# Two weight conversions moved by one batch each, and vector work queued behind the softmax low part

## The chip, the cores and the metric

One NeuronCore of a Trainium2 chip runs the kernel. The metric is device time in microseconds (us); lower is better. The time of a kernel is the median of its runs.

## The reference

Four batches (B = 4) of 576 tokens go through an attention with 32 memory slots and then through two feed-forward networks, all in fp32.

```python
# attention, 8 heads of 64
a = softmax(phi)                       # over 32 memory slots
k_m, v_m = a^T k, a^T v                # 32 x 64 per head
attn = softmax(q k_m^T / 8)
x = (attn v_m) as (2304 tokens, 512)
# first network
h = max(x @ moe_w_in, 0);   x = (h * h) @ moe_w_out
# second network
h = x @ moe2_w_in
g = h * tanh(log1p(exp(min(h, 20))))   # for h > 20: h * tanh(h)
out = g @ moe2_w_out
```

Both `w_in` are 512 x 2048, both `w_out` 2048 x 512.

## The kernel before

**Numbers in two parts.** Every large matrix product is made as three products of parts: a high part (rounded to the type that TensorE multiplies fast) and a low part (what the rounding left). high x high, high x low and low x high add up in PSUM; so each product shows three lines of matmuls (L471 to L473 for the first layer of network one, L433 to L435 for its second layer, L780 to L782 and L755 to L757 for network two).

**Weights have to be converted.** The four weight matrices arrive as 64-bit words. The class `Conv` turns them, in units of 128 x 512 values, into fp32 (and into high and low part). Network one's are called i1 and o1, network two's i2 and o2, 16 units each. A unit takes three ticks. In the first, ScalarE scales the high word in place (L192, the Prelu). In the second, VectorE joins the words (L214, L221, into `ct`), the raw buffer comes free and the next raw load is issued (L167). In the third, ScalarE rounds (L187) and VectorE makes the low part (L229). i2 and o2 are then stored to DRAM scratch from a staging tile (L231) and loaded again later (L713, `load_w2`), since SBUF has no room for them yet. The staging tiles have the tag `i1` with 4 buffers, which is also the tag of the pages of w_in1 that are loaded again for later batches (L592, `win1r`).

**Stages.** Attention (`kv_unit`, `attn_unit`) makes, for each batch and half batch of 288 tokens, the softmax part `at` (VectorE transpose L368), its high part `ah` (ScalarE, L375) and its low part `al` (VectorE, L376). `w_part` multiplies v_m into w_in1 (L386) and splits the result (`wp`, L392 and L393), so that the first layer reads ah, al and wp directly. `a_tile` runs the first network: for each of up to 16 blocks of d_ff (a step) six matmuls to `h`, ScalarE Relu (L479) and Square (L480), high part `g` (L484, or on VectorE for batch 3, L486), low part (L487, VectorE), and 12 matmuls that add to four accumulators, three steps later (`LAG`). Batches 0 and 1 are taken together in groups of 4, 6 and 6 blocks, 12 calls of `a_tile` numbered i = 0 to 11; the batches numbered 2 and 3 (the third and the last) follow with 16 blocks for each half. The second network then takes all tokens in 5 tiles of 512 or 384.

**Order.** A planner orders the instructions of each engine beforehand, from the order in which the code names them and from its own estimates of when operands are ready; an instruction may be moved far ahead of its place in the code. An engine then executes strictly in that order. `tc.issue_after(x)`, here in `behind(marks, key)`, keeps the instructions of its block behind x on x's engine, and adds no wait for anything else. `marks[b, half]` is a VectorE instruction of the softmax of that half batch. `c1.after` names the mark behind which the joining work of `Conv.fields` stays, for i1 and o1: (0,0) up to i = 0, (0,1) at i = 1, (1,0) at i = 2, (1,1) at i = 3 and none after. `kv_soft` puts the batch 2 maximum (L260) behind (1,1). `paced` puts the Prelu behind the latest Relu named (`marks["step"]`). All DMAs are issued by SyncE's queue, SP, one after another.

`c2` is the converter of the second network's weights: i2 and then o2, one unit started in two of three ticks, from the third group of batches 0 and 1 (once c1 is done) to the end of batch 2. While batch 3 runs, the 16 units of i2 and then those of o2 are loaded into their final places.

Of the kernel before, what the change touches and what calls it, by code (L numbers as in the profile page):

```python
# [8 lines left out]
F32 = mybir.dt.float32  # L9
F32R = mybir.dt.float32r  # L10
# [7 lines left out]
B, H, S, D, M = 4, 8, 576, 64, 32  # L18
DM, FF = 512, 2048
P = 128  # L20
# [4 lines left out]
NF = FF // P  # L25
# [4 lines left out]
LAG = 3  # L30
# [5 lines left out]
def body(tc, q, kvm, kvt, phi, w_in1, w_out1, w_in2, w_out2, out):  # L36
    nc = tc.nc
# [13 lines left out]
    dram = cm_dram.__enter__()  # L51
    cm_const, const = open_pool("const", "left")
    cm_wo, wo = open_pool("wo", "left")
    cm_pg, PG = open_pool("pg", "left")
    cm_x, X = open_pool("x", "left")
    cm_y, Y = open_pool("y", "right")
# [11 lines left out]
    for p in range(2):  # L68
        t = Y.tile([P, (NC + 1) * P], F32, name=f"phi{p}")
# [62 lines left out]
    wt = {}  # L132

    w1 = dram.tile([NPG, P, 4, 256], F32, name="w_i1")
    w2 = {key: dram.tile([NF, P, 2, 512], F32, name=f"w_{key}") for key in ("i2", "o2")}

    marks = {}
# [10 lines left out]
    class Conv:  # L150
# [20 lines left out]
        def tick(self, start=True, between=None):  # L171


            ends = [x for x in self.flight if x[2] == 2]
            bits = [x for x in self.flight if x[2] == 1]
            for x in ends:
                key, u = x[0], x[1]
                if key[1] == "2":
                    x[4] = Y.tile([P, 2, 512], F32R, tag="i1", name=f"st_{key}_{u}", bufs=4)
                    x[4] = [x[4][:, 0], x[4][:, 1], x[4]]  # L180
                else:
                    if (key, u // 2) not in wt:
                        wt[key, u // 2] = tuple(
                            wo.tile([P, 2, DM], F32R, tag=f"wo{part}{u // 2}", name=f"{key}{part}{u // 2}")
                            for part in "hl")
                    x[4] = [w[:, u % 2, :] for w in wt[key, u // 2]]
                nc.scalar.copy(x[4][0], x[3])  # L187
            if start and self.started < min(self.loaded, self.limit) and self.ready(*self.order[self.started]):
                key, u = self.order[self.started]
                high = self.raw[key, u][:, :, 1].bitcast(F32)  # L190
                with behind(marks, "step" if self.paced else None):
                    nc.scalar.activation(high, high, AF.Prelu, scale=2.0 ** -112, alpha=-2.0 ** 32)  # L192
                self.started += 1
                self.flight.append([key, u, 0, None, None])
            with behind(marks, self.after):
                self.fields(bits, ends, between)
            for x in self.flight:
                x[2] += 1
            for x in list(self.flight):
                if x[2] == 3 or (x[2] == 2 and x[0] == "i1"):  # L200
                    self.done.add((x[0], x[1]))
                    self.flight.remove(x)

        def fields(self, bits, ends, between):
            for x in bits:
                key, u, c = x[0], x[1], x[1] % 2
                if key == "i1":
                    if c == 0:
                        wt[key, u // 2] = Y.tile(
                            [P, 4, 256], F32, tag="i1", name=f"win1_{u // 2}", bufs=4)  # L210
                    x[3] = wt[key, u // 2][:, :, c * P:(c + 1) * P]
                else:
                    x[3] = X.tile([P, 512], F32, tag="ct", name=f"ct_{key}_{u}", bufs=2)
                nc.vector.tensor_scalar(  # L214
                    out=x[3].bitcast(I32), in0=self.word(x, 0), scalar1=29, scalar2=None,
                    op0=ALU.logical_shift_right)
            if between is not None:
                between()
            for x in bits:
                d = x[3].bitcast(I32)  # L220
                nc.vector.scalar_tensor_tensor(  # L221
                    out=d, in0=self.word(x, 1), scalar=3, in1=d,
                    op0=ALU.logical_shift_left, op1=ALU.bitwise_or)
                if x[0] == "i1" and x[1] % 2:
                    nc.sync.dma_start(w1[x[1] // 2], wt["i1", x[1] // 2])
                self.raw.pop((x[0], x[1]))
                self.load()
            for x in ends:
                nc.vector.tensor_sub(x[4][1], x[3], x[4][0].bitcast(F32))  # L229
                if x[0][1] == "2":  # L230
                    nc.sync.dma_start(w2[x[0]][x[1]], x[4][2].bitcast(F32))  # L231

        def word(self, x, i):
            t = self.raw[x[0], x[1]][:, :, i]
# [104 lines left out]
    def attn_unit(b, half, nxt=None):  # L339
        n = f"{b}{half}"  # L340
        qt = q_t.pop((b, half))
        ps = banks2(f"psc{n}")
        for g in range(4):
            for p in range(2):
                done_pe["psc", b, half] = nc.tensor.matmul(
                    ps[M * g:M * g + M, p, :T], kT[b][D * p:D * p + D, M * g:M * g + M],
                    qt[g // 2][D * p:D * p + D, g % 2, :], start=True, stop=True)
        if nxt is not None:
            nxt()

        x = Y.tile([P, 2, T], F32, tag="x", name=f"x{n}", bufs=1)
        xv = x.rearrange("p a (c m) -> p (a c) m", m=NB)
        for p in range(2):
            nc.vector.transpose(x[:, p], ps[:, p, :T])
        mx = Y.tile([P, 2 * TB], F32, tag="smx", name=f"smx{n}", bufs=1)
        marks[b, half] = nc.vector.tensor_reduce(out=mx, in_=xv, op=ALU.max, axis=AX.X)
        yield
        nc.vector.tensor_sub(xv, xv, mx.unsqueeze(2).to_broadcast([P, 2 * TB, NB]))
        nc.scalar.activation(x, x, AF.Exp)
        yield  # L360
        sm = Y.tile([P, 2 * TB], F32, tag="ssm", name=f"ssm{n}", bufs=1)
        nc.vector.tensor_reduce(out=sm, in_=xv, op=ALU.add, axis=AX.X)
        nc.vector.tensor_scalar_add(sm, sm, EPS)
        nc.vector.reciprocal(sm, sm)
        nc.vector.tensor_mul(xv, xv, sm.unsqueeze(2).to_broadcast([P, 2 * TB, NB]))
        yield
        a = Y.tile([P, 2, T], F32, tag="at", name=f"at{n}", bufs=1)
        marks[b, half] = nc.vector.transpose(  # L368
            a.rearrange("p a t -> p (a t)"), x.rearrange("p a t -> p (a t)"))
        pool = Y if b in (1, 2) else X  # L370
        a_t[b, half] = tuple(
            pool.tile([P, 2, T], F32R, tag=f"a{part}", name=f"a{part}{b}{half}", bufs=2)
            for part in "hl")
        hi, lo = a_t[b, half]
        nc.scalar.copy(hi, a)  # L375
        nc.vector.tensor_sub(lo, a, hi.bitcast(F32))  # L376
        yield

    wp = {}
# [116 lines left out]
    bounds = [sum(GROUPS[:i]) for i in range(len(GROUPS) + 1)]  # L496
# [73 lines left out]
    def attn_later(b, half):  # L570
        def nxt():
# [11 lines left out]

    subs = [(f0, f1, b, half) for f0, f1 in zip(bounds, bounds[1:])
            for b in range(2) for half in range(2)]
    c2 = Conv([("i2", u) for u in range(NF)] + [("o2", u) for u in range(NF)],
              lambda i: (Y, "raw", 3))

    def load_page(j):

# [4 lines left out]
    for i, (f0, f1, b, half) in enumerate(subs):  # L595
        final = i == len(subs) - 1
# [25 lines left out]
        def tick(fc):  # L622
            if len(c1.done) < 2 * NF:
                c1.tick()
            elif f0 == bounds[-2]:
                if not c2.loaded:
                    c2.load(3)
                c2.tick(start=fc % 3 != 2)

        def mid(fc):  # L630
            run_step(lanes, n_steps)
# [29 lines left out]


    def tick2(fc):
        c2.tick(start=fc % 3 != 2)

    b, nb = 2, 3
    lanes = [attn_later(b, 1), [[iter(range(2)), 2]] + kv_later(nb)]
# [25 lines left out]
    drain(*lanes)  # L693


    while len(c2.done) < 2 * NF:
        c2.tick()
    close(cm_psum2)
    cm_psum2 = tc.tile_pool(name="psum3", bufs=1, space=PSUM)
# [5 lines left out]
        tiles.append((c, n))  # L705
        c += n

    def load_w2(key, u):
        if key == "i2":
            t = Y2.tile([P, 2, 512], F32R, name=f"i2_{u}")  # L710
        else:
            t = wo.tile([P, 2, 512], F32R, tag=f"wo{'hl'[u % 2]}{u // 2}", name=f"o2_{u}")
        nc.sync.dma_start(t.bitcast(F32), w2[key][u])  # L713
        wt[key, u] = t

    y_raw, y_t = {}, {}

# [12 lines left out]
        nc.scalar.copy(hi, t)  # L730
        (nc.gpsimd if i else nc.vector).tensor_sub(lo, t, hi.bitcast(F32))  # L731

    def post0(fc):
        load_w2("i2", fc)

    def post1(fc):
        if fc >= 8 and fc % 2 == 0:
            load_y(0, fc // 2 - 4)
        elif fc >= 8:
            split_y(0, fc // 2 - 4)  # L740
        if fc >= LAG + 1 and fc % 2 == 0:
            load_w2("o2", fc - LAG - 1)
            load_w2("o2", fc - LAG)

    nothing = lambda fc: None
    acc_tags = ["mm", "b0", "bg1", "bg2"]
    a_tile(B - 1, 0, 0, NF, nothing, nothing, post0, acc_tags)
    a_tile(B - 1, 1, 0, NF, nothing, nothing, post1, acc_tags)


    def mm4_step(acc, fc, gh, gl, n, done):
# [18 lines left out]
    for i, (c0, n) in enumerate(tiles):  # L770
        acc = [psum.tile([P, 512], F32, tag=f"acc{d}", name=f"b{i}{d}") for d in range(n // P)]
        done = store_out(c0)
        for fc in range(NF):
# [9 lines left out]
            if step == 1:  # L783
                flush()
                run_pend(0)
                for c in range(NF):
                    if ("o2", c) not in wt:
                        load_w2("o2", c)
            u = X.tile([P, 512], F32, tag="ah", name=f"u{m}", bufs=2)[:, :n]
            nn = X.tile([P, 512], F32, tag="al", name=f"n{m}", bufs=2)[:, :n]  # L790
            nh = X.tile([P, 512], F32, tag="ys0", name=f"nh{m}", bufs=2)[:, :n]
# [80 lines left out]
```

## Time and profile before

| | |
|---|---|
| median of 3 runs | 811.53 us (810.93 to 815.98) |
| profiled execution | 809.73 us, its span 807.9 us |
| TensorE matmul (PE) busy | 776.5 us, 96% |
| VectorE (DVE) busy | 577.8 us, 72% |
| ScalarE (ACT) busy | 452.3 us, 56% |
| mean granted TensorE clock | 0.983 |
| DMA, mean | 138 GB/s over the span |

The profile is of one execution. The span runs from the first to the last instruction. PE, DVE, ACT and POOL are the busy rows of TensorE's matmuls, VectorE, ScalarE and GpSimd; PEclk is the granted TensorE clock, 1.00 being the upper of its two levels (2.4 GHz) and 0.50 the lower (1.2 GHz). A gap in front of an instruction is shown in brackets with what ended it.

### The profile page before, as it was taken

To read this page: it belongs to the slowest core of one execution; us is meant where nothing else is said; L and a number is where in the kernel's file an instruction comes from. 1 tells how busy PE (TensorE), PEld (TensorE's weight loads), DVE (VectorE), ACT (ScalarE), POOL (GpSimd) and SP (SyncE) were. 2 spreads that over 40 slices of the span, in tenths; PEclk is the share of its full clock that TensorE was granted. 3 is DMA by queue.
4 is the path that set the end of the run, shared out by engine and by line. 5 is a ranking of instruction groups with operands and counts; after the bars stand their busy time and mean duration, and the time that the engine had idled before them with its cause. 6 is when DMAs were issued, how large, how long until landed. Compare 5 with 4: busy or idle time off the path is not lost.

```text
span 807.9 us, 13777 instructions
## 1 busy us (share of the span) xinstructions
PE 776.5 (96%) x5288; PEld 676.5 (84%) x5288; DVE 577.8 (72%) x1022; ACT 452.3 (56%) x916; POOL 119.4 (15%) x104
## 2 busy tenths in 40 slices
PE   5797999999988999999999999999999999999997
PEld 4586898999777988999988888888888889999896
DVE  4988646785677883334588887888878887777774
ACT  3767766785657775334445445444564446555453
POOL 0000000000000000000223243222522242222222
PEclk7698999999999999999999999999999999999999
DMA  9991435699789977506630002000110001001001
GB/s 337 406 391 73 164 100 162 235 329 362 251 312 345 389 253 281 211 1 228 248 105 1 0 27 73 0 1 1 39 53 1 0 20 54 1 1 39 1 2 39
DMA packets 38705, 111.77 MB, mean 138 GB/s; under 512 B 3952, under 2 KB 10096, under 8 KB 38640
## 3 DMA queue, kind: packets, MB, share of 16 engines
q1 hardware_dynamic: 38640, 110.90, 37.8%
q8 instruction: 41, 0.67, 0.3%
q14 instruction: 24, 0.20, 0.1%
HBM read 80.48 MB, written 30.41 MB: 137 GB/s over the span
## 4 chain that ended last, share of the span: by engine, by line
PE 80%; DMA 8%; DVE 7%; ACT 3%; issue 1%; SPq 0%; ACTq 0%; DVEq 0%
PE hb L781 8%; PE hb L780 8%; PE hb L782 8%; PE b L756 8%; PE b L755 8%; PE b L757 8%; PE a L433 6%; PE a L435 6%; PE a L434 6%; DMA raw_i<-in_moe_w_in_dram 3%; PE h L471 3%; PE h L472 3%; PE h L473 3%; DMA w_i<-st_i 2%; PE pw L386 1%
## 5 line engine op out<-in xcount | busy, mean ns | idle before, releaser
L433 PE MATMUL a<-g,o1h 128*128 128x288 f32 x512 | 150.3, 301 | 3.0 <-ACT g L484 1.5
L434 PE MATMUL a<-g,o1l 128*128 128x288 f32 x512 | 149.2, 297 | 0.0
L808 POOL TENSOR_TENSOR gl<-nh,gh 128x512 fp32r<-128x512 f32 (+1 forms) x80 | 97.4, 1219 | 285.5 <-PE b L757 177.0
L435 PE MATMUL a<-g,o1h 128*128 128x288 f32 x512 | 134.8, 295 | 0.7 <-DVE g L487 0.7
L781 PE MATMUL hb<-yl,i 128*128 128x512 f32 (+1 forms) x320 | 118.9, 372 | 0.0
L780 PE MATMUL hb<-yh,i 128*128 128x512 f32 (+1 forms) x320 | 118.9, 372 | 0.0
L782 PE MATMUL hb<-yh,i 128*128 128x512 f32 (+1 forms) x320 | 118.8, 371 | 0.0
L804 DVE SCALAR_TENSOR_TENSOR n<-n,u 128x512 f32<-128x512 f32 (+1 forms) x80 | 79.5, 994 | 52.5 <-ACT u L800 52.5
L756 PE MATMUL b<-o,gh 128*128 128x512 f32 x288 | 113.6, 395 | 0.0
L755 PE MATMUL b<-o,gh 128*128 128x512 f32 x288 | 113.5, 394 | 0.0
L757 PE MATMUL b<-o,gl 128*128 128x512 f32 x288 | 112.4, 395 | 0.0
L433 PEld LDWEIGHTS a<-g,o1h 128*128 128x128 f32 x512 | 96.5, 189 | 11.1 <-ACT g L484 4.0
L794 ACT ACTIVATE u<-hb 128x512 f32<-128x512 f32 (+1 forms) x80 | 44.4, 555 | 107.5 <-PE hb L782 107.5
L434 PEld LDWEIGHTS a<-g,o1l 128*128 128x128 f32 x512 | 96.8, 189 | 1.3 <-issue 1.2
L479 ACT ACTIVATE s<-h 128x288 f32<-128x288 f32 x128 | 52.0, 410 | 79.9 <-PE h L473 78.4
L435 PEld LDWEIGHTS a<-g,o1h 128*128 128x128 f32 x512 | 90.7, 188 | 3.0 <-DVE g L487 1.6
L471 PE MATMUL h<-ah,wp 128*128 128x288 f32 x256 | 79.9, 313 | 5.3 <-ACT s L479 2.6
L472 PE MATMUL h<-al,wp 128*128 128x288 f32 x256 | 77.8, 304 | 5.3 <-DVE al L376 5.3
L487 DVE TENSOR_TENSOR g<-s,g 128x288 fp32r<-128x288 f32 x128 | 59.9, 469 | 32.2 <-ACT g L484 30.3
L731 POOL TENSOR_TENSOR yl<-yr,yh 128x512 fp32r<-128x512 f32 (+1 forms) x16 | 21.3, 1345 | 396.2 <-PE h L473 391.4
L807 ACT CAST gh<-nh 128x512 fp32r<-128x512 f32 (+1 forms) x80 | 46.3, 579 | 57.4 <-DVE nh L806 54.3
L473 PE MATMUL h<-ah,wp 128*128 128x288 f32 x256 | 77.1, 301 | 0.0
(98 smaller groups left out, 1393.4 us busy)
## 6 DMA issues: line engine op xcount, KB each, us to landing
raw_i<-in_moe_w_in_dram SPq DMA_DIRECT2D x32, 512.0 KB, 5.2
raw_o<-in_moe_w_out_dram SPq DMA_DIRECT2D x32, 512.0 KB, 7.7
win1r<-w_i SPq DMA_DIRECT2D x17, 512.0 KB, 5.8
w_i<-st_i SPq DMA_DIRECT2D x16, 512.0 KB, 4.5
w_o<-st_o SPq DMA_DIRECT2D x16, 512.0 KB, 6.8
i<-w_i SPq DMA_DIRECT2D x16, 512.0 KB, 7.7
o<-w_o SPq DMA_DIRECT2D x16, 512.0 KB, 4.1
kv<-in_kvm_dram SPq DMA_DIRECT2D x5, 1024.0 KB, 8.8
```

The costliest lines, as they stand in the source:

```text
L433: nc.tensor.matmul(o, wh[:, c, cs], sh, start=first, stop=False)
L434: nc.tensor.matmul(o, wl[:, c, cs], sh, start=False, stop=False)
L435: nc.tensor.matmul(o, wh[:, c, cs], sl, start=False, stop=last)
L471: nc.tensor.matmul(ph, w[:, 0, hg, fs], hi[:, hg], start=(hg == 0), stop=False)
L472: nc.tensor.matmul(ph, w[:, 0, hg, fs], lo[:, hg], start=False, stop=False)
L473: nc.tensor.matmul(ph, w[:, 1, hg, fs], hi[:, hg], start=False, stop=(hg == 1))
L755: nc.tensor.matmul(acc[t], gh[:, cs], wh, start=(fc == 0), stop=False)
L756: nc.tensor.matmul(acc[t], gh[:, cs], wl, start=False, stop=False)
L757: nc.tensor.matmul(acc[t], gl[:, cs], wh, start=False, stop=(fc == NF - 1))
L780: nc.tensor.matmul(h, wh[:, d * P:d * P + P], yh, start=(d == 0), stop=False)
L781: nc.tensor.matmul(h, wh[:, d * P:d * P + P], yl, start=False, stop=False)
L782: nc.tensor.matmul(h, wl[:, d * P:d * P + P], yh, start=False, stop=(d == 3))
```

## The change

- `c2` now holds o2 alone. Its first three raw loads are issued at the start of the last `a_tile` of batches 0 and 1 (i = 11); units start only in batch 2, one in every second step. Its staging is now two tiles of 128 x 512, high and low, with the tags `ys2` and `ys3` (2 buffers each; batches 0 and 1 used them for their sums), and each is stored by a DMA of its own (256 KB).
- A new converter `c3` holds i2. It runs during batch 3, one unit in every second step, with raw buffers in the pool `Y2`, and writes high and low part straight into the final tile. i2 is neither stored to scratch nor loaded from it.
- Both are `paced`.
- `marks[b, half]` is now the low part `al` (L376) and not the transpose (L368).

```diff
-    w2 = {key: dram.tile([NF, P, 2, 512], F32, name=f"w_{key}") for key in ("i2", "o2")}
+    w2 = dram.tile([NF, P, 2, 512], F32, name="w_o2")
...
-                if key[1] == "2":
-                    x[4] = Y.tile([P, 2, 512], F32R, tag="i1", name=f"st_{key}_{u}", bufs=4)
-                    x[4] = [x[4][:, 0], x[4][:, 1], x[4]]
+                if key == "i2":
+                    t = wt[key, u] = Y2.tile([P, 2, 512], F32R, name=f"i2_{u}")
+                    x[4] = [t[:, 0], t[:, 1]]
+                elif key == "o2":
+                    x[4] = [Y.tile([P, 512], F32R, tag=f"ys{i}", name=f"st{i}_{u}", bufs=2) for i in (2, 3)]
...
-                if x[0][1] == "2":
-                    nc.sync.dma_start(w2[x[0]][x[1]], x[4][2].bitcast(F32))
+                if x[0] == "o2":
+                    for i in range(2):
+                        nc.sync.dma_start(w2[x[1], :, i], x[4][i].bitcast(F32))
...
-        marks[b, half] = nc.vector.transpose(
-            a.rearrange("p a t -> p (a t)"), x.rearrange("p a t -> p (a t)"))
+        nc.vector.transpose(a.rearrange("p a t -> p (a t)"), x.rearrange("p a t -> p (a t)"))
...
-        nc.vector.tensor_sub(lo, a, hi.bitcast(F32))
+        marks[b, half] = nc.vector.tensor_sub(lo, a, hi.bitcast(F32))
...
-    c2 = Conv([("i2", u) for u in range(NF)] + [("o2", u) for u in range(NF)],
-              lambda i: (Y, "raw", 3))
+    c2 = Conv([("o2", u) for u in range(NF)], lambda i: (Y, "raw", 3))
+    c3 = Conv([("i2", u) for u in range(NF)], lambda i: (Y2, "raw", 3))
+    c2.paced = c3.paced = True
...
-            elif f0 == bounds[-2]:
-                if not c2.loaded:
-                    c2.load(3)
-                c2.tick(start=fc % 3 != 2)
+            elif final and not c2.loaded:
+                c2.load(3)
...
     def tick2(fc):
-        c2.tick(start=fc % 3 != 2)
+        c2.tick(start=fc % 2 == 0)
...
+    c3.load(3)
+
+    def tick3(fc):
+        c3.tick(start=fc % 2 == 0)
...
-    a_tile(B - 1, 0, 0, NF, nothing, nothing, post0, acc_tags)
-    a_tile(B - 1, 1, 0, NF, nothing, nothing, post1, acc_tags)
+    a_tile(B - 1, 0, 0, NF, tick3, nothing, nothing, acc_tags)
+    a_tile(B - 1, 1, 0, NF, tick3, nothing, post1, acc_tags)
+    while len(c3.done) < NF:
+        c3.tick()
```

## Rows read from the trace of the kernel before

**Rows 1.** The page, its first part: busy us of each engine.
```profile
PE 776.5 (96%) x5288; PEld 676.5 (84%) x5288; DVE 577.8 (72%) x1022; ACT 452.3 (56%) x916; POOL 119.4 (15%) x104
```

**Rows 2.** Busy time by stretch; after the engines PEclk, DMA share, GB/s.
```profile
70.00:80.00 10.00, 5.40 (x25) 4.93 (x24) 9.31 (x23) 6.19 (x15) 0.00 (x0) 0.67 0.02 8
170.00:262.00 92.00, 83.84 (x834) 74.15 (x833) 63.75 (x132) 60.36 (x137) 0.00 (x0) 1.00 0.90 324
221.50:320.00 98.50, 92.56 (x916) 82.22 (x917) 70.25 (x139) 68.10 (x154) 0.00 (x0) 1.00 0.86 318
320.00:400.00 80.00, 80.00 (x608) 79.15 (x593) 31.88 (x74) 33.42 (x78) 5.22 (x4) 1.00 0.48 172
```

**Rows 3.** Timeline of PE, 200 to 262 us: start, duration, gap and its releaser.
```profile
204.98 0.72 PE L345 MATMUL psc<-q,kT 64*32 64x288 f32 x16 [0.37 <-ACT kT L319]
...
221.53 0.40 PE L471 MATMUL h<-ah,wp 128*128 128x288 f32 x1 [1.09 <-ACT ah L375]
...
229.22 0.37 PE L433 MATMUL a<-g,o1h 128*128 128x288 f32 x1 [1.22 <-ACT st_i L187]
...
233.68 0.40 PE L433 MATMUL a<-g,o1h 128*128 128x288 f32 x1 [1.45 <-ACT g L484]
...
243.93 0.67 PE L386 MATMUL pw<-win1r,vT 64*32 64x256 f32 x16 [1.04 <-ACT et L282]
...
258.54 0.40 PE L471 MATMUL h<-ah,wp 128*128 128x288 f32 x1 [2.21 <-ACT s L479]
```

**Rows 4.** Timeline of ACT, the same stretch.
```profile
220.29 0.62 ACT L187 CAST st_i<-ct_i 128x512 fp32r<-128x512 f32 x1 [3.05 <-DMA win1r<-w_i]
...
240.38 0.68 ACT L192 ACTIVATE raw_o<-raw_o 128x512 f32<-128x512 f32 x1 [2.27 <-DMA raw_o<-in_moe_w_out_dram]
...
255.82 0.62 ACT L187 CAST st_o<-ct_o 128x512 fp32r<-128x512 f32 x1 [3.83 <-DMA w_o<-st_o]
```

**Rows 5.** DMAs of the scratch tensor w_o: issue in ns min/median/max, landing in us.
```profile
L231 SPq DMA_DIRECT2D w_o<-st_o x16: 319/327/2389, 233.6 to 299.2; - x16
...
DMA to landing us min/median/max: 3.0/4.9/9.6
```

**Rows 6.** Groups by line: the five instructions of a unit, total us, mean ns.
```profile
L221 DVE SCALAR_TENSOR_TENSOR ct_o<-raw_o,ct_o 128x512 int32<-128x512 int32 x32 | 22.0, 689 | 4.8 <-ACT raw_o L192 4.3
...
L192 ACT ACTIVATE raw_o<-raw_o 128x512 f32<-128x512 f32 x32 | 21.6, 674 | 9.4 <-DMA raw_o<-in_moe_w_out_dram 9.3
...
L214 DVE TENSOR_SCALAR ct_o<-raw_o 128x512 int32<-128x512 int32 x32 | 13.5, 422 | 6.4 <-DMA raw_o<-in_moe_w_out_dram 6.3
...
L229 DVE TENSOR_TENSOR st_o<-ct_o,st_o 128x512 fp32r<-128x512 f32 x16 | 11.0, 685 | 6.1 <-ACT st_o L187 5.9
...
L187 ACT CAST st_o<-ct_o 128x512 fp32r<-128x512 f32 x16 | 10.0, 624 | 7.3 <-DMA w_o<-st_o 4.5 <-DMA w_i<-st_i 2.7 <-DVE x L365 0.2
```

**Rows 7.** Timeline of ACT, DVE and PE, 70 to 81 us (softmax of batch 1, second half).
```profile
70.24 0.67 ACT L375 CAST ah<-at 128x576 fp32r<-128x576 f32 x1 [0.74 <-DVE at L368]
...
74.92 0.75 DVE L376 TENSOR_TENSOR al<-at,ah 128x576 fp32r<-128x576 f32 x1
...
80.16 0.45 DVE L487 TENSOR_TENSOR g<-s,g 128x288 fp32r<-128x288 f32 x1
...
75.72 0.61 PE L472 MATMUL h<-al,wp 128*128 128x288 f32 x1 [4.23 <-DVE al L376]
```

**Rows 8.** Busy time from the end of the transpose to the start of al.
```profile
70.10:74.90 4.80, 1.02 (x6) 0.55 (x4) 4.80 (x11) 3.13 (x8) 0.00 (x0) 0.85 0.00 0
```

**Rows 9.** The chain of waits behind that gap: start, share on the chain, what.
```profile
76.33 0.24 PE h L473
...
79.93 0.24 PE h L471
...
80.53 0.13 PE h L471
```

**Rows 10.** Timeline of ACT and PE, 21 to 25 us (softmax of batch 0, first half).
```profile
21.44 0.67 ACT L375 CAST ah<-at 128x576 fp32r<-128x576 f32 x1
...
24.13 0.61 PE L472 MATMUL h<-al,wp 128*128 128x288 f32 x1 [1.10 <-DVE al L376]
```

More of the change, by code (lines that the diff above doesn't have):

```diff
@@ L693, in body @@
     drain(*lanes)
-    while len(c2.done) < 2 * NF:
+    while len(c2.done) < NF:
         c2.tick()
@@ L706, in body, with load_w2 @@
         c += n
[L708 to L714, printed above, removed]
+    def load_w2(u):
+        t = wo.tile([P, 2, 512], F32R, tag=f"wo{'hl'[u % 2]}{u // 2}", name=f"o2_{u}")
+        nc.sync.dma_start(t.bitcast(F32), w2[u])
+        wt["o2", u] = t
+    c3.load(3)
+    def tick3(fc):
+        c3.tick(start=fc % 2 == 0)
     y_raw, y_t = {}, {}
@@ L731, in split_y @@
         (nc.gpsimd if i else nc.vector).tensor_sub(lo, t, hi.bitcast(F32))
-    def post0(fc):
-        load_w2("i2", fc)
     def post1(fc):
@@ L741, in post1 @@
         if fc >= LAG + 1 and fc % 2 == 0:
-            load_w2("o2", fc - LAG - 1)
-            load_w2("o2", fc - LAG)
+            load_w2(fc - LAG - 1)
+            load_w2(fc - LAG)
     nothing = lambda fc: None
     acc_tags = ["mm", "b0", "bg1", "bg2"]
-    a_tile(B - 1, 0, 0, NF, nothing, nothing, post0, acc_tags)
-    a_tile(B - 1, 1, 0, NF, nothing, nothing, post1, acc_tags)
+    a_tile(B - 1, 0, 0, NF, tick3, nothing, nothing, acc_tags)
+    a_tile(B - 1, 1, 0, NF, tick3, nothing, post1, acc_tags)
+    while len(c3.done) < NF:
+        c3.tick()
     def mm4_step(acc, fc, gh, gl, n, done):
@@ L787, in body @@
                     if ("o2", c) not in wt:
-                        load_w2("o2", c)
+                        load_w2(c)
             u = X.tile([P, 512], F32, tag="ah", name=f"u{m}", bufs=2)[:, :n]
```

## The prediction

> **What bounds the kernel now.** The page's busy times come first [rows 1]: TensorE's matmuls fill 776.5 of the 807.9 us span, so time can only come from the 31.4 us in which PE is not busy, and from stretches at a lower clock. Where these lie is read from the busy times by stretch [rows 2]. Two stretches matter. From 70 to 80 us PE is busy for 5.40 of 10 us and the granted clock is 0.67. From 170 to 262 us PE is busy for 83.84 of 92 us, 8.16 us of gaps at a clock of 1.00. From 320 to 400 us, which is batch 3, PE has no gap at all.
>
> The timeline of PE shows what ends the gaps of the second stretch [rows 3]: 1.09, 1.22, 1.45, 1.04 and 2.21 us, each ended by a ScalarE instruction, though ScalarE is busy for only 60.36 of the 92 us [rows 2]. So ScalarE was held up, and its own timeline shows by what [rows 4]: the rounding L187 waited 3.05 us for a page load and 3.83 us for a store, because its staging tile shares four buffers with these, and the Prelu waited 2.27 us for a raw load. ScalarE works in order: Relu and the high part of g stand behind such a wait, and PE runs dry when its lead of three steps is used up.
>
> The first stretch is one wait [rows 7]: the matmul with al starts after a gap of 4.23 us. The high part ah had ended at 70.24 + 0.67 = 70.91 us, but VectorE took al up only at 74.92, having been busy without a break from the transpose on [rows 8] with ten other instructions: joining work of the conversion, two maxima of batch 2, a split of wp, a copy. After the gap the matmuls on the chain lie 0.24 us apart up to about 80.2 us, then 0.13 [rows 9]: the lower of the two clock levels, 1.2 GHz.
>
> **i2 taken out of batches 0 to 2.** Out go sixteen stores and sixteen loads of 512 KB through scratch, with their issues on SP; the raw loads stay and move. What is left beside batch 2 is o2. Its staging no longer waits for a page load, nor a page load for it, and a unit starts every two steps, with raw loads three units ahead and the Prelu behind a Relu. In batch 2 two steps take 98.5 / 16 = 6.16 us [rows 2], or 92.56 / 16 = 5.79 without the gaps. So a raw load has some 17 us, a staging tile, of which there are two pairs, 11.6 us until it is needed again. A scratch DMA took 4.9 us in the median and 9.6 at worst [rows 5]; rounding and low part before it take 0.62 + 0.69 = 1.31 [rows 6]. A median cycle of 6.2 us fits into 11.6. Of the 8.16 us of gaps 0.37 belongs to the attention's kT [rows 3] and stays: 7.8 can go. The least is the two gaps behind waits for raw loads, 1.22 + 1.04 = 2.3. I take 7.0, near the upper end, since every long gap has one of these two causes, and leave 0.8 for the DMA queue, which is still well used (share 0.90 now, [rows 2]). No clock is regained here: it was 1.00 throughout.
>
> The DMA issues of o2 stay at 32 on SP, since 16 of i2 are replaced by the second halves. They stand on SP before the page loads, the attention's loads and later raw loads; the longest issue now is 2.4 us [rows 5], against 5.79 us for a pair of steps.
>
> **i2 beside batch 3.** A unit costs ScalarE 0.67 + 0.62 = 1.30 us and VectorE 0.42 + 0.69 + 0.69 = 1.80 [rows 6]. Sixteen add 20.8 and 28.8 us. From 320 to 400 us ScalarE has 33.4 and VectorE 31.9 of 80 busy [rows 2]: 54 and 61 afterwards, below PE's 80. What hides the work is PE's own, with a lead of three steps; if the first raw load were late, the Prelu at the head would hold Relu, and that cover is the first to go. The loads replace others of the same size. The last unit ends after the last step and its weights are used only in the sixteenth step of the next stage. I cost it at nothing, and up to 1.5 us (a unit's 1.30 plus hand-over) at the other end.
>
> **al ahead of the other vector work.** In the first stretch al can end at about 70.91 + 0.75 = 71.7 instead of 75.67: 4.0 us off the gap. The copy and the wp split are not bound by the new edge, but fit into the 0.8 us in which VectorE waits for ah. If the gap shrinks that far, the clock need not fall: 17 matmuls at 0.24 instead of 0.13 cost 1.8 us [rows 9]. So 5.8 us at best. Against it stand the ten instructions, 4.8 us of VectorE time [rows 8], that now stand behind al. PE has 24 matmuls of `h` at 0.13, 3.2 us, before it needs anything more; then the low part of g, whose first one ended at 80.61 [rows 7]. If VectorE keeps the order of the rest, that hardly moves, and the gain is about 0.5 us. One conversion unit for each step is what the code asks for (1.80 us), and the maxima belong to batch 2 and can go later, so most of it need not stand ahead of g. I take 4.0, nearer the upper end.
>
> At the start VectorE will now wait for ah, from the transpose's end to 21.44 + 0.67 = 22.11 us [rows 10], some 0.9 us in which it did joining work before. In exchange PE's wait of 1.10 us for al shrinks. Between a loss of 0.9 and a gain of 1.1 I take nothing. The other two half batches of this part had no PE wait for al; an idle moment of VectorE there is covered by queued matmuls.
>
> **Sum.** 7.0 + 4.0 = 11.0 us. The profiled execution took 809.73 us, 1.83 more than its span and 1.80 less than the median of the runs, 811.53. So 798.7 against the profiled execution and 800.5 against the median. My forecast is 800.5 us.
>
> **Rivals.**
>
> *The wait moves from al to the low part of g.* For it: VectorE is busy 9.31 of 10 us from 70 to 80 [rows 2]; what is pushed back has to be done some time. Against it: it is mostly not yet due. Then only 0.5 of the 4.0 comes, 804.0 us. Chance 0.19.
>
> *The mark does not do what it says.* An edge orders VectorE only; if the planner lets ah itself come later, or moves unbound work in front, al stays late, and the start pays 0.9. Against it: ah ran right after its operand [rows 7]. Gain 7.0 - 0.9: 805.4 us. Chance 0.10.
>
> *The staging becomes the bound of batch 2, slower than before.* Two pairs of places replace four shared ones. With the worst landing, 9.6 us, and the longest issue, 2.4, a cycle is 1.31 + 2.4 + 9.6 = 13.3 us, so 6.65 us for a unit: 16 units take 106.4 us where batch 2 took 98.5 [rows 2]. That is 7.9 more; 4.0 for al and about 1.8 for gaps ahead of batch 2 come off: 813.6 us. It decides once the mean cycle passes 11.6 us. For it: the share of the DMA engines is 0.86 over batch 2 now. Against it: the median landing is half of what is needed, and one unit in two steps is a quarter less traffic than two in three. Chance 0.11, in a third of it with SP blocked for longer still, over 1% slower.
>
> The Trainium skill, page "DMA: Bandwidth & Descriptors", section "Anatomy of one DMA", speaks against the split store: it gives each DMA a fixed 2.0 us (measured there on GpSimd's path) beside a term for bytes. By its figures two stores of 256 KB one after another come to an estimate of 5.2 us against 3.2 for one of 512 KB. By that the cycle would be 6.5 us, and this rival's time would not arise at all; no run here shows a store of this size into scratch, and the landings in the rows, up to 9.6 us for 512 KB, are well above the page's figure, so its chance is kept.
>
> **Numbers.** The forecast's own case has the remaining 0.60. Its range reaches from all gains at their upper ends, 7.8 + 5.8 + 1.1 = 14.7 us, so 796.8 us by the median and 795.0 by the profiled execution, to about 804. The range to hold 8 in 10 goes on over the first two rivals, with the 1.5 us of batch 3 and lower ends of the gaps, to 809.5, and leaves out the third and a little below: 794.5 to 809.5. One per cent, about what a measurement of this kernel tells from no change, is 8.1 us: faster means below 803.4, slower above 819.6. The own case is nearly all faster, and about a quarter of the first two rivals: 0.65. Slower by over 1% is a third of the third rival and a rest for a planner's order that turns out badly: 0.06. Within 1% is 0.29.
>
> **What would show it.** Right: no gap of PE over 0.5 us between 170 and 262 us with a ScalarE releaser; L187 without DMA waits; al starting within 1 us after ah; a clock near 1.00 from 70 to 80 us; batch 3 without gaps and VectorE near 61 of 80 us there. Wrong: L187 waiting for stores of w_o; a new gap of PE ended by L487 near 75 us; a Prelu of i2 waiting for its load at the start of batch 3, or gaps before 40 us larger than now.

## The result, and the profile after

The changed kernel takes 801.12 us in the median of 4 runs (799.52 to 801.88), the kernel before, beside it, 811.23 us: a ratio of 0.9861, 95% interval 0.982 to 0.9902. The forecast was 800.5 us. The profiled execution took 800.84 us, its span 799.0 us.

Busy time by stretch of the changed kernel, with the columns of [rows 2]; the row before the last covers the gaps of [rows 3], the last is most of batch 3.

```profile
70.00:80.00 10.00, 8.49 (x80) 6.63 (x79) 9.61 (x22) 8.15 (x20) 0.00 (x0) 1.00 0.05 19
80.00:90.00 10.00, 9.27 (x79) 8.23 (x77) 8.42 (x19) 8.13 (x20) 0.00 (x0) 1.00 0.63 190
90.00:100.00 10.00, 8.46 (x62) 7.37 (x63) 6.40 (x14) 6.15 (x16) 0.00 (x0) 0.83 0.48 162
170.00:262.00 92.00, 91.34 (x941) 81.16 (x939) 53.45 (x112) 54.93 (x125) 0.00 (x0) 1.00 0.71 228
311.00:387.00 76.00, 76.00 (x578) 76.00 (x575) 52.23 (x118) 46.55 (x103) 0.00 (x0) 1.00 0.59 199
```

From 170 to 262 us 0.66 us of gaps are left of 8.16. Batch 3 has none, with VectorE at 52 and ScalarE at 47 of 76 us. From 70 to 80 us the clock is 1.00 where it was 0.67. But from 80 to 100 us PE is now busy for 17.7 of 20 us, and the clock falls to 0.83 in the second half. In the kernel before PE had no gap there:

```profile
80.00:90.00 10.00, 10.00 (x82) 8.85 (x82) 8.64 (x18) 9.17 (x24) 0.00 (x0) 0.99 0.60 201
90.00:100.00 10.00, 10.00 (x80) 8.85 (x79) 5.25 (x12) 6.62 (x17) 0.00 (x0) 1.00 0.46 162
```

The timeline of PE, 60 to 100 us (all gaps that it lists there), and the one gap that it lists from 160 to 400 us:

```profile
71.99 0.54 PE L473 MATMUL h<-ah,wp 128*128 128x288 f32 x2 [0.68 <-ACT ah L377]
72.79 0.40 PE L474 MATMUL h<-al,wp 128*128 128x288 f32 x1 [0.26 <-DVE al L378]
78.88 0.67 PE L388 MATMUL pw<-win,vT 64*32 64x256 f32 x16 [0.43 <-DVE win L223]
88.69 0.40 PE L473 MATMUL h<-ah,wp 128*128 128x288 f32 x1 [0.48 <-ACT s L481]
91.54 0.40 PE L473 MATMUL h<-ah,wp 128*128 128x288 f32 x1 [1.79 <-ACT s L481]
...
202.34 0.72 PE L348 MATMUL psc<-q,kT 64*32 64x288 f32 x16 [0.37 <-ACT kT L322]
```

(Two or three lines were added ahead of these, so L473 to L475 answer to L471 to L473 before, L378 to L376, L194 to L192, L189 to L187, L223 to L221.) The gap of 4.23 us in front of al [rows 7] is 0.26 us. Three gaps are new: 0.43 us behind VectorE's joining of a w_in1 page (`win`, L223), and 0.48 and 1.79 us, both ended by Relu. The chain of waits of the changed kernel shows where the longer one comes from (start, share on the chain, what):

```profile
82.51 0.69 DVE ct_o L223
83.20 0.60 DVE wp L395
83.80 0.33 DVE ct_o L216
84.13 0.61 DVE win L223
84.74 0.02 issue
84.76 5.41 DMA raw_o<-in_moe_w_out_dram
90.17 0.02 issue
90.19 0.03 ACT raw_o L194
90.21 0.56 issue
90.77 0.42 ACT s L482
91.19 0.31 ACT s L481
91.50 0.04 issue
91.54 0.40 PE h L473
```

Read from the bottom: PE waits for Relu (L481), which stands on ScalarE behind a Square (L482) and a Prelu (L194); the Prelu waits for a raw load of 5.41 us; and that load was issued only when a piece of VectorE's joining work was done at 84.74 us. The load itself is no later than before: counted from the start of this half batch's transpose it was issued after 14.6 us in the kernel before (84.01 us) and 14.3 here. But there it landed after 3.8 us, and its Prelu ran 20.6 us after the transpose, held up by PE's own wait for al; here the Prelu is due earlier, and the load lands at 19.7. PE has come nearer to joining work and loads that did not get faster.

The staging: DMAs of w_o in the changed kernel (32 stores of 256 KB and the loads), as in [rows 5], and what ScalarE's rounding L189 waited for (us in total, times).

```profile
L234 SPq DMA_DIRECT2D w_o<-st x32: 319/320/989, 217.8 to 306.4; - x32
...
DMA to landing us min/median/max: 2.0/5.1/7.9
```

```profile
DVE ct_i L223: 3.5, 8
DVE ct_o L223: 1.9, 2
DMA w_o<-st: 0.2, 1
```

These medians, 5.1 us and 4.9 before, are over the stores and the later loads of that tensor. For the stores alone (KB each, median us from issue to landing; before, then after):

```profile
w_o<-st_o SPq DMA_DIRECT2D x16, 512.0 KB, 6.8
w_o<-st SPq DMA_DIRECT2D x32, 256.0 KB, 4.8
```

A half store thus lands 2.0 us sooner than a whole one did, with less traffic beside it, and ScalarE waited for one only once, for 0.2 us.

Where the time went, by the start of the same event in both profiles (us):

| event | before | after | difference |
|---|---|---|---|
| second kk transpose of batch 0 | 19.22 | 19.45 | +0.23 |
| score matmuls, batch 1, first half | 48.29 | 49.67 | +1.38 |
| first matmul with al, batch 1, second half | 75.72 | 72.79 | -2.93 |
| `pw` matmuls of `w_part` near 139 us | 139.56 | 138.57 | -0.99 |
| score matmuls, batch 2, first half | 204.98 | 202.34 | -2.64 |
| first g of batch 3 | 322.32 | 312.97 | -9.35 |
| first matmul of network two | 396.77 | 387.39 | -9.38 |

So 1.1 us were lost at the start and 4.3 us won up to the matmul with al. By 139 us 1.0 us of that lead is left: the new gaps and the lower clock behind them took the rest, and the gain of clock behind al too. The stretch from there to batch 2, in which the conversion of i2 had begun beside the third group, is 1.65 us shorter (63.8 against 65.4 us); the gaps that went there, 0.43 and 0.25 us, show 0.7 of it. 6.7 us came from batch 2. By the end of the span 0.5 us of the 9.4 are lost again.

### The profile page after: what moved, and what is told of

The parts are those of the page before. It is cut to its first block, busy times and chain, and to the rows that moved or that the text cites. A ratio compares the mean times of both kernels' runs of the same rounds, so it can differ in the third digit from the quotient of the medians.

```text
span 799.0 us, 13701 instructions
## 1 busy us (share of the span) xinstructions
PE 776.2 (97%) x5288; PEld 676.5 (85%) x5288; DVE 573.0 (72%) x1022; ACT 453.4 (57%) x916; POOL 119.8 (15%) x104
## 4 chain that ended last, share of the span: by engine, by line
PE 88%; DVE 3%; DMA 3%; ACT 3%; issue 1%; SPq 0%; ACTq 0%; DVEq 0%
PE hb L783 8%; PE hb L782 8%; PE hb L784 8%; PE b L758 8%; PE b L757 8%; PE b L759 8%; PE a L435 8%; PE a L436 8%; PE a L437 8%; PE h L473 4%; PE h L474 4%; PE h L475 4%; PE pw L388 2%; DMA raw_i<-in_moe_w_in_dram 2%; PE pk L306 1%
## 5 line engine op out<-in xcount | busy, mean ns | idle before, releaser
L806 DVE SCALAR_TENSOR_TENSOR n<-n,u 128x512 f32<-128x512 f32 (+1 forms) x80 | 75.2, 940 | 54.5 <-ACT u L802 54.5
L481 ACT ACTIVATE s<-h 128x288 f32<-128x288 f32 x128 | 52.5, 412 | 74.6 <-PE h L475 70.6
L489 DVE TENSOR_TENSOR g<-s,g 128x288 fp32r<-128x288 f32 x128 | 57.6, 452 | 42.4 <-ACT g L486 39.9
L473 PE MATMUL h<-ah,wp 128*128 128x288 f32 x256 | 79.4, 311 | 5.9 <-ACT wp L394 2.8
L475 PE MATMUL h<-ah,wp 128*128 128x288 f32 x256 | 76.3, 299 | 0.7 <-DVE wp L395 0.7
```

Source lines behind the costliest of these rows:

```text
L473: nc.tensor.matmul(ph, w[:, 0, hg, fs], hi[:, hg], start=(hg == 0), stop=False)
L475: nc.tensor.matmul(ph, w[:, 1, hg, fs], hi[:, hg], start=False, stop=(hg == 1))
```

## The experiments

Ratios are to the kernel before, run beside each kernel in one of four sets: the changed kernel, the first four experiments, the next four, and the last four. The kernel before had medians of 811.23, 811.71, 811.74 and 811.51 us in them, so medians of different sets can be compared to about 0.5 us.

**The marks alone.** On the kernel before:

```diff
-        marks[b, half] = nc.vector.transpose(a..., x...)
+        nc.vector.transpose(a..., x...)
-        nc.vector.tensor_sub(lo, a, hi.bitcast(F32))
+        marks[b, half] = nc.vector.tensor_sub(lo, a, hi.bitcast(F32))
```

> Kernel before with the marks alone moved to the low part al. Theory: the marks give little on balance, 1.1 us lost at the start, 3.9 us won at the gap of batch 1's second half and 1.8 us of clock behind it, and some 3 to 4 us given back between 80 and 100 us where the joining work that was pushed back comes due: 2 us faster than before, 809.2 us. Rival A, the marks carry most of the change: 804 to 806 us. Rival B, with i2 and o2 still beside batches 0 to 2 nothing is left of it: 811 us.

Measured: 809.02 us, ratio 0.9969 (0.9949 to 0.999). The total is as the theory had it; rival A is out, and rival B, no change, lies just outside the interval. In its trace PE waits 0.26 us for al, and gaps of 0.56 and 1.92 us stand near 88 and 91 us, the clock from 90 to 100 us being 0.66. The two new gaps thus belong to the marks and not to the moved conversions. The theory's sum is not borne out in this trace, though: from the second kk transpose to the score matmuls of batch 2 it takes 186.0 us, and 185.8 in the kernel before. What the marks won had been lost by there, and the gain of the profiled execution came later.

**The conversions alone.** The changed kernel with `marks[b, half] = nc.vector.transpose(...)`.

> The changed kernel with the marks put back on the transpose. Theory: the conversions carry 7.0 to 7.9 us, the gaps that PE had behind ScalarE from 170 to 262 us: 803.5 to 804 us, with the gap of 4.2 us and the lower clock at 70 to 80 us back. Rival A: 807 us. Rival B: 801 us.

Measured: 801.53 us, ratio 0.9881 (0.9858 to 0.9904), more than expected and nearly the whole change; it is rival B's number. In its trace the stretch from 170 to 262 us has 0.56 us of gaps, and the gap in front of al is back:

```profile
76.40 0.61 PE L475 MATMUL h<-al,wp 128*128 128x288 f32 x1 [4.23 <-DVE al L379]
```

Between the score matmuls of batch 2 and batch 3's first g it takes 110.5 us, the kernel before 117.3: 6.9 us less. The stretch ahead of it, from the `pw` matmul near 139 us, takes 63.8 us as in the changed kernel, and 65.6 us with the marks alone. So 8.5 us can be seen in the trace, as much as the two profiled executions differ by. The ratio says 9.7 us, between 7.8 and 11.5.

**The last mark alone, and all but the first.** Both on the changed kernel:

```diff
+        low = nc.vector.tensor_sub(lo, a, hi.bitcast(F32))
+        if (b, half) == (1, 1):        # the other kernel: != (0, 0)
+            marks[b, half] = low       # else the transpose, as before
```

> The changed kernel, but the mark is the low part only for batch 1's second half; the three earlier half batches keep the transpose. Theory: VectorE's wait for ah at the start is the loss there, so 1.1 us comes back and the later gain stays: 800.0 us, the score matmuls of batch 1's first half near 48.3 us instead of 49.7. Rival: the later start in that profile was not made by the mark, or the time is taken up by the backlog at 80 to 100 us: 801.1 us, no change.

> As the changed kernel, but the very first half batch keeps the transpose as its mark. Theory: the first edge alone makes the loss, so this is as the kernel with the edge of batch 1's second half alone: 800.0 us. Rival: the middle two edges matter too, each shifting VectorE by the 0.4 to 0.8 us in which it waits for ah while it is nearly full: 800.5 to 801 us.

Measured: 795.72 us (ratio 0.9798, 0.9773 to 0.9823) and 798.96 us (0.9838, 0.9811 to 0.9865). Against the conversions alone, the last mark by itself is worth 801.53 - 795.72 = 5.8 us. That is more than the theory gave it: without the other three marks the loss at the start is gone and also the later gaps, which I had put to the last mark. PE's gaps from 60 to 100 us with the last mark alone:

```profile
70.33 0.53 PE L476 MATMUL h<-ah,wp 128*128 128x288 f32 x2 [0.36 <-ACT ah L378]
71.23 0.40 PE L477 MATMUL h<-al,wp 128*128 128x288 f32 x1 [0.37 <-DVE al L379]
77.09 0.67 PE L391 MATMUL pw<-win,vT 64*32 64x256 f32 x16 [0.24 <-DVE win L223]
```

With the middle two marks as well, the gaps near 90 us are there again:

```profile
87.56 0.40 PE L476 MATMUL h<-ah,wp 128*128 128x288 f32 x1 [0.50 <-ACT s L484]
90.38 0.40 PE L476 MATMUL h<-ah,wp 128*128 128x288 f32 x1 [1.76 <-ACT s L484]
```

So the middle marks cost 3.2 us, though no matmul had waited for their al. From the matmul with al to the score matmuls of batch 2 the traces differ by 2.4 us, of which these two gaps are 2.3. The raw load behind them and its Prelu, first with the last mark alone, then with the middle two as well:

```profile
82.98 0.33 SPq L167 DMA_DIRECT2D raw_o<-in_moe_w_out_dram  x1
87.37 0.70 ACT L194 ACTIVATE raw_o<-raw_o 128x512 f32<-128x512 f32 x1
...
83.60 0.33 SPq L167 DMA_DIRECT2D raw_o<-in_moe_w_out_dram  x1
89.03 0.68 ACT L194 ACTIVATE raw_o<-raw_o 128x512 f32<-128x512 f32 x1 [1.52 <-DMA raw_o<-in_moe_w_out_dram]
```

Counted from the transpose the load is issued 14.2 and 14.3 us on, so it is not issued late. But the raw load ahead of it goes out 0.7 us later with the middle marks (12.8 against 12.1 us on), and this one then takes 5.4 us instead of 4.1 to land. That the one makes the other is likely and not shown. The planner also put one Relu more ahead of this Prelu with the last mark alone; what that is worth is open. The rival of the second expectation held, and its price was too low. The first mark costs what remains to the changed kernel, a ratio of 0.9861 against 0.9838, 1.9 us, though the intervals overlap. From the second kk transpose to the score matmuls of batch 1 it takes 30.2 us with it and 29.1 without. The traces differ by another 1.5 us behind the gaps near 90 us, which were followed by a lower clock in the changed kernel and not in this one.

**Shared staging.** The changed kernel with o2 staged as before:

```diff
-  x[4] = [Y.tile([P, 512], F32R, tag=f"ys{i}", name=f"st{i}_{u}", bufs=2) for i in (2, 3)]
+  x[4] = Y.tile([P, 2, 512], F32R, tag="i1", name=f"st_{u}", bufs=4)
+  x[4] = [x[4][:, 0], x[4][:, 1], x[4]]
...
-  for i in range(2):
-      nc.sync.dma_start(w2[x[1], :, i], x[4][i].bitcast(F32))
+  nc.sync.dma_start(w2[x[1]], x[4][2].bitcast(F32))
```

> The changed kernel, but o2 is staged again in the four buffers that it shares with the pages of w_in1, 512 KB in one store. Theory that both the move of i2 and the places matter: most of the gaps of PE between 200 and 262 us come back, ScalarE's rounding waits for stores and page loads again: 4 to 6 us over the changed kernel, 805 to 807 us. Rival, the move of i2 (less traffic, one unit in two steps, the Prelu paced) is enough and the places add nothing: within 1 us of 801 us, no gap of PE over 0.5 us there.

Measured: 805.01 us, ratio 0.991 (0.9876 to 0.9945), its runs spread from 800.85 to 808.48. By the median the places are worth 3.9 us, but the interval overlaps that of the changed kernel (0.982 to 0.9902). The profiled execution was the quickest, no slower than the changed kernel, so its trace shows the waits and not what the slower runs lost by them. It shows no gap from 200 to 262 us but that for kT (0.36 us), so the place I named was wrong; they come later, near 288 to 306 us (1.07, 0.48 and 1.38 us). Waits of ScalarE for DMAs of w_o from 200 to 320 us (total, times, longest):

```profile
ACT st L190 <- DMA w_o<-st: 8.0, 5, 3.5
```

**Half of the staging.** One pair of places: `tag="ys2"` for both parts.

> The changed kernel with half of the staging: one pair of places for high and low part instead of two. A store then has to land before the next unit is rounded. With 1.3 us for rounding and low part and a store of about 4.8 us the cycle is 6.1 to 6.5 us against 5.8 for two steps. Theory, the staging decides only past that point, and a little late is covered by the lead of three steps: 1 to 8 us slower than the changed kernel, 802 to 809 us, with waits of L189 for w_o. Rival, the staging is nowhere near a bound: 801 us, L189 hardly waits. Rival the other way, the bound of batch 2: over 811 us.

Measured: 803.47 us, ratio 0.9888 (0.9858 to 0.9919), by the medians 2.4 us slower than the changed kernel, with overlapping intervals. PE has four new gaps in batch 2, 3.1 us together. ScalarE's wait, same view:

```profile
ACT st L189 <- DMA w_o<-st: 9.4, 5, 3.4
```

Near the point at which staging decides, it costs little; the second pair is enough to be rid of it.

**The maxima later.** The changed kernel, with `marks["gl"]` set to the low part of g (L489) in each step:

```diff
-        with behind(marks, (1, 1) if b == 2 else None):
+        with behind(marks, "gl" if b == 2 else None):
```

> The changed kernel, but the two maxima of batch 2 stay behind the low part of g named last, so that they run near 190 us and not at 74 to 76 us. That takes 1.3 us of VectorE and 2 us of ScalarE out of the stretch in which the joining work comes due. Theory, the backlog of joining work makes the two gaps of PE near 88 and 91 us: they shrink, and with them the low clock behind them: 797 to 799 us. Rival, the gaps come from raw loads that stand in SP's queue behind a store of a w_in1 page, whatever VectorE does besides: 801 us.

Measured: 797.94 us, ratio 0.9817 (0.9787 to 0.9847). The gaps near 90 us are gone:

```profile
80.00:90.00 10.00, 10.00 (x77) 8.27 (x76) 9.03 (x20) 8.48 (x23) 0.00 (x0) 1.00 0.68 205
90.00:100.00 10.00, 10.00 (x78) 10.00 (x77) 4.44 (x10) 6.29 (x17) 0.00 (x0) 1.00 0.30 112
```

So 1.3 us of VectorE work and 2 us of ScalarE's, not due for another 100 us, were what tipped it. The same raw load is now issued 12.6 us after the transpose and lands at 17.0; its Prelu still waits 1.22 us, but early enough for PE not to feel it. The backlog is the cause; which of the two engines' share tipped it is not shown, since this edit moves both.

**Page stores from another queue.** The changed kernel with the stores of w_in1 pages issued by GpSimd: `nc.gpsimd.dma_start(w1[x[1] // 2], ...)`.

> The changed kernel, but the stores of the joined pages of w_in1 are issued by GpSimd's queue and not by SP's, where one waited 15.5 us for its page between 63 and 79 us with the raw loads behind it. Theory, raw loads that come late behind that store make the gap at 91 us (the Prelu waited 1.54 us for one): gaps near 88 and 91 us gone, 797 to 799 us. Rival, the raw loads wait for their buffers, that is for the joining work itself, not for the store: 801 us and the same gaps.

Measured: 800.44 us, ratio 0.9853 (0.9824 to 0.9883). The gaps stay, 1.5 us in sum where they were 2.3; the raw load behind them is issued 14.3 us after the transpose as before. The store ahead of the raw loads is not the cause by itself: they wait for their buffers.

```profile
90.22 0.40 PE L473 MATMUL h<-ah,wp 128*128 128x288 f32 x1 [0.88 <-ACT s L481]
91.90 0.40 PE L473 MATMUL h<-ah,wp 128*128 128x288 f32 x1 [0.61 <-ACT s L481]
```

**Edits together.** The last mark alone with the maxima later; all marks but the first with the maxima later; and the conversions alone (all marks on the transpose) with the maxima later.

> The two edits that helped together: the mark is the low part only for batch 1's second half, and the maxima of batch 2 stay behind the low part of g named last. If both act by the same backlog, the second adds nothing where the first has already removed the gaps near 90 us: 795 to 796 us. If the maxima still cost something, 794 us. Rival, the two do not combine and the planner's order turns out worse: over 797 us.

> The maxima later, and the low part as mark for the three half batches after the first. Theory: the first edge costs 0.8 us at the start, so 0.8 to 1 us under the kernel with all edges and later maxima: 797.0 us. The middle two then cost only what is left of the backlog: within 1.5 us of the kernel with the last edge alone. Rival, the first edge's price of some 2 us in the medians is real without any gap behind it: 796 us.

> The conversions as changed, all marks on the transpose, the maxima later. The maxima were 1.3 of the 4.8 us of vector work ahead of the low part. Theory, the gap is made by all that stands ahead: it shrinks from 4.2 to about 2.9 us, and the low clock behind it may go: 1.3 to 3.1 us under the kernel with the conversions alone, 798.4 to 800.2 us. Rival, the planner fills their place with other joining work: 801.5 us and a gap of 4.2 us.

Measured: 796.23 us (ratio 0.9799, 0.977 to 0.9828), 795.99 us (0.9802, 0.9772 to 0.9832) and 800.05 us (0.9851, 0.9824 to 0.9878). The first two equal the last mark alone: the two cures act on one backlog and do not add. The second is 2.0 us under the kernel with all marks and later maxima by the medians (797.94 - 795.99) and 1.2 us by the ratios, so it does not part the theory from the rival. The traces do: from the second kk transpose to the score matmuls of batch 1 it takes 29.1 to 29.2 us in all seven kernels without the first mark and 30.1 to 30.2 us in six of the seven with it. The seventh is the kernel with all marks and later maxima, 31.2 us. The first mark's price is thus 1.1 us, and that one execution lost another 1.0 us. In the third the gap in front of al shrinks by the 1.3 us of the maxima, as expected of a gap that is the sum of what stands ahead:

```profile
74.59 0.40 PE L475 MATMUL h<-al,wp 128*128 128x288 f32 x1 [2.91 <-DVE al L379]
```

**No pace.** The changed kernel without `c2.paced = c3.paced = True`.

> The changed kernel with the Prelu of o2 and i2 not held behind a Relu. Theory, the pace adds nothing, since raw loads run three units ahead: 801 us, no wait of the Prelu for a raw load that PE feels. Rival, the planner moves the Prelus far ahead and ScalarE waits at them for loads again, as for i2 before: gaps of PE between 200 and 320 us of 2 us or more in sum, 803 us and up.

Measured: 800.95 us, ratio 0.9863 (0.9828 to 0.9897): the pace adds nothing that shows. Three gaps of 0.40, 0.40 and 0.66 us appear in batch 2 and leave the total alone.

The lowest median is that of the changed kernel with the last mark alone, 795.72 us: about 2% under the kernel before, and 0.6% under the changed one by the ratios. The first two of the edits together are not told apart from it.

## Why the prediction was right, point by point

**The total** came out 0.6 us from the forecast, but of its two terms one was too small and one too large. That they cancel so nearly is luck.

**i2 out of batches 0 to 2, 7.0 us: the mechanism right, the size too small.** The gaps from 170 to 262 us are gone but for 0.66 us, and ScalarE's rounding waited for a DMA only once, for 0.2 us. In the trace 8.4 us can be seen (6.7 in batch 2 and 1.7 ahead of it), above the 7.8 that I had held for the most. I had counted gaps alone, and about 1 us of the stretch ahead of batch 2 stood in no gap that the profile lists; what it was stays open. The conversions alone brought 9.7 us by the ratio. The staging cycle was rightly judged, on a misread row: the 4.9 us of [rows 5] is over stores and later loads, and the stores alone took 6.8. A cycle of 8.1 us fits into 11.6 too. With two pairs next to nothing waits; with one pair (a cycle of 6.1 us against 5.8 for two steps) 2.4 us are lost by the medians. Shared places give back 3.9 us of the median, so the places and the move of i2 seem both to count.

**i2 beside batch 3 at nothing: right.** There is no gap, and VectorE and ScalarE are less busy than worked out: 52 and 45 of 80 us from 320 to 400 us against 61 and 54. In part this is because profiled instructions of one engine overlap here by about 0.1 us (joining instructions of 0.68 us start every 0.60 us), which a sum of mean durations counts twice: about 4.8 us for VectorE's 48 instructions and 3.2 for ScalarE's 32. The rest was not traced.

**al ahead of the other work, 4.0 us: the step itself was right, its size as part of the whole wrong.** al starts less than 0.1 us after its operand is ready, the gap is closed, and the clock stays at 1.00 from 70 to 80 us. That step alone is worth 5.8 us (the last mark alone), the upper end that I had worked out. With all four marks it is worth between nothing and 1.6 us: 801.12 us against 801.53 for the conversions alone by the medians, 0.9861 against 0.9881 by the ratios. Two steps of mine failed. I let the other two half batches cost nothing, because no matmul had waited there; they cost 3.2 us, for the most part in gaps behind raw loads 30 to 50 us further on, one of which landed 1.4 us later. And I balanced the start at zero, between a loss of 0.9 and a gain of 1.1; it costs 1.1 us in the traces, more than the loss that I allowed for. The sign that I had named for this came: from 20 to 50 us PE's gaps sum to 5.7 us, and to 4.9 before.

**The rival "the wait moves"** had the right idea of the backlog and the wrong place: not the low part of g at 75 us but a raw load at 85 us, whose issue waits for the joining that frees its buffer, and then Prelu, Square, Relu and PE in a row. VectorE does take up the low part of g in time (no gap was ended by it there). The rival of the staging and the one of the mark without effect did not come.

**The Trainium skill's page "DMA: Bandwidth & Descriptors"**, section "Anatomy of one DMA", gave an estimated 5.2 us for two half stores one after another, 2.6 for each. Here one half store took 4.8 us in the median and 7.9 at worst, about twice the estimate. But the second goes out 0.5 to 1.9 us behind the first in 15 of the 16 units, so that both are in flight together, and a pair had landed 5.8 us after its first issue in the median (3.0 to 9.9). The estimate was near for the pair, though not for the reason that it gives, and the rival that it spoke against did not show.

## What to carry to other kernels

An order edge moves a whole class of work, not only the piece that blocked: put it on the one place where a wait shows (here one mark of four) and price the others by what they push back, up to the loads that wait for buffers this work frees. When a gap closes, ask what the engine now reaches earlier: here PE came to a raw load that was issued no later than before. A gap made by work that stands ahead on a full engine shrank one for one with that work (4.23 to 2.91 us for 1.3 us), so look first for work there that is not due for long. Staging that shares buffers with unrelated loads ties two queues together; two pairs of places of its own removed a wait that four shared ones had.

## What the runs showed of the hardware that was not expected

The same gaps of about 0.5 and 1.8 us near 88 and 91 us were followed by a granted clock of 0.83 in the changed kernel (90 to 100 us) and 0.66 with the marks alone, but by 1.00 in the kernel without the first mark, where the stretch from al's matmul to the next ones behind these gaps is 1.5 us shorter than in the changed kernel; before, a gap of 2.21 us at 258 us had left it at 1.00. And behind the gap of 4.23 us in front of al the mean clock from 70 to 80 us was 0.67 in the kernel before and 0.83 with the conversions alone, the matmuls returning to 0.13 us at 80.2 us in the one and 79.4 us in the other. A gap's price in clock was thus not the same from one profiled execution to another; no run here shows what decides it.
